# SyncE's transfers of the first stage: five under way at most, and a warm-up of two wide products

## The chip, the cores and the metric

One core of one Trainium2 chip runs the kernel. TensorE (PE in the profile, its weight loads PEld), VectorE (DVE), ScalarE (ACT) and GpSimd (POOL) compute; SyncE (SP) issues nearly all transfers, and sixteen DMA engines carry them. The metric is the device time of one execution in microseconds, lower is better.

## What is computed

A batch of 2 sequences of 3008 tokens with 256 features is filtered in the frequency domain, and two MLP layers follow, token by token. In float32:

```python
X = np.fft.rfft(x, axis=1)
y = np.fft.irfft(X * (filt_r + 1j * filt_i)[None], n=3008, axis=1)
t = y.reshape(6016, 256)
g = t @ w_gate                                    # 256 -> 1536
t = (g / (1 + np.exp(-g)) * (t @ w_val)) @ w_out  # 1536 -> 256
h = t @ w_in                                      # 256 -> 2048
out = (h * np.clip(h + 3, 0, 6) / 6) @ w_out2     # 2048 -> 256
```

The two MLPs' weights are held in float64; the kernel reads their words and makes float32 values of them.

## The kernel before

**Three stages on one core.** The first, about the first 72 us, is the Fourier part: 3008 = 47 x 64, so the transform is a product over 47 (`over_n1`), one over 64 (`over_n2`), the product with the filter (`filter_product`), and the way back over 64 (`back`); the way back over 47 (`to_time`) stands at the seam to the MLP. The second, to about 165 us, runs the first MLP for the first 1024 tokens, and meanwhile decodes its weights. The third, the rest, runs units of 7 products of 512 columns for the first MLP of the other tokens and then the second MLP.

**The first stage step by step.** It has 16 steps `STEPS`, each of 16 times 8 channels of one batch. Step k runs, in the order of the code, `over_n1(k)` (64 matmul records, line 332), `back(k-2)` (16 records, line 374), the transfers that `moves` holds for k, `over_n2(k)` (16 records, line 348) and `filter_product(k)` (four products on DVE, line 361, and four sums on POOL). `back(k-2)` needs those sums of step k-2. ACT takes results out of PSUM (lines 339, 340, 379). DVE also multiplies the filters' imaginary part by a sign (`prepare_filter`, line 324) and decodes the first weights (`Decode.part`, lines 196 to 209) between the steps.

**What SP issues in the first stage.** The matrices `mat`; the inputs `load_x(k)`, two transfers of 256 KB each into a ring of four places `ring`, issued three steps ahead; the filters `load_filter(j)`, two of 192 KB; the weights `load_dec(f)`, three of 256 KB or one of 768 KB; the results `store(b, a, i)`, 192 KB each from `turned` to the scratch `d2` in DRAM; and from there `load_half`, which brings back the halves that `form` turns to time (`g<-d`, `y<-d`, `turned<-d`). `load_x(0)` alone goes through ACT's queue. In the second stage `low_w1` stores decoded weights (`w1f<-x`) and `store` the other batch.

**What sets the order.** The engines' order is that of the code (a manual schedule). A transfer's landing is told by one of eight semaphores (DMAHW0 to DMAHW7) that are used in turn, so a transfer also waits until the eighth last has landed. SP takes its transfers in order: what stands behind a waiting one waits too.

**The warm-up.** Before the first input has landed, `idle(8)` multiplies a blank tile of 128 x 128 (line 317), which DVE has set to zero (line 311), eight times.

Of the kernel before, what the change touches and what calls it, by code (L numbers as in the profile page):

```python
# [16 lines left out]
P = 128  # L17
B, S, D = 2, 3008, 256
N1, N2 = 47, 64
N1P = 48  # L20
# [57 lines left out]
def fft_conv_glu_mlp(ctx: ExitStack, tc: tile.TileContext, x, filt, mats, sgn, w1, w2, out):  # L78
    nc = tc.nc
    w1, w2 = w1.bitcast(U32), w2.bitcast(U32)  # L80
# [9 lines left out]
    sg = keep.tile([P, NK], F32, name="sg")  # L90
# [7 lines left out]
    def wall(f):  # L98
        return wall_a[:, f] if f < 8 else wall_b[:, f - 8]


    d2 = [dram.tile([NK, P, D], F32, name=f"d2_{b}") for b in range(B)]
    yd = [dram.tile([P, 4, 512], F32, name=f"yd_{k}") for k in range(len(BLOCKS))]
    w1f = [dram.tile([P, 10 * P], F32, name=f"w1f_{f}") for f in range(F1)]
# [5 lines left out]
    def bank(tag="gv"):  # L110
        turn[tag] += 1
        return banks[tag][(turn[tag] - 1) % 4]

    def minus(out, a, b, engine=None):
        (engine or nc.vector).tensor_tensor(out=out, in0=a, in1=b, op=ALU.subtract)  # L115
# [9 lines left out]
    def rows(i, n=64):  # L125

        return slice(i * 64, i * 64 + n)
# [4 lines left out]
    def turns(first, n):  # L132

        return 32 * first // N1, -(-(32 * first + n // 2) // N1)
# [132 lines left out]
    with tc.manual_schedule():  # L267
# [7 lines left out]
        fl = [a[:, :3072].rearrange("p (j r n) -> p j r n", j=4, r=2) for a in (x0, side)]  # L275
        ring = work.tile([P, 7168], F32, tag="xs", name="ring")
        turned = work.tile([P, 7168], F32, tag="xs", name="turned")[:, :6144].rearrange("p (b q c) -> p b q c", b=2, c=P)
        room = new_y()

        N, RING = 16, 2  # L280
        STEPS = [(b, 4 * a + i) for a in range(2) for b in range(B) for i in range(4)]
        xin, first, spec, acc2 = {}, {}, {}, {}

        def load_x(k, engine=nc.sync):
            b, j = STEPS[k]
            if k % 2 == 0:
                xin[k // 2] = ring[:, k // 2 % RING * 2048:(k // 2 % RING + 1) * 2048].rearrange("p (a n) -> p a n", a=2)
            to, src = (v.rearrange("p (o i n) -> p i o n", o=2, i=2) if k < 2 else v.rearrange("p (i n) -> p i n", i=2)
                       for v in (xin[k // 2][:, k % 2], x[b, j // 2, :, j % 2]))
            for i in range(2):  # L290
                engine.dma_start(out=to[:, i], in_=src[:, i])

        def load_filter(j):
            for r in range(2):
                nc.sync.dma_start(out=fl[j // 4][:, j % 4, r], in_=filt[j][:, r])

        load_x(0, nc.scalar)
        load_x(1)
        nc.sync.dma_start(out=sg, in_=sgn)
        load_filter(0)  # L300
        load_filter(1)
        load_x(2)
        load_filter(2)
        load_x(3)
        load_filter(3)
# [1 line left out]
        nc.gpsimd.memset(warm, 0.0)  # L307
        nc.scalar.activation(out=warm, in_=warm, func=AF.Silu)

        blank = turned[:, 1, 0]  # L310
        nc.vector.memset(blank, 0.0)

        def idle(n):

            acc = bank()
            for _ in range(n):
                nc.tensor.matmul(acc[:, :P], blank, blank)

        idle(8)

        def prepare_filter(j):

# [57 lines left out]

        def store(b, a, i):
            q = slice(i * NK // 8, (i + 1) * NK // 8)
            nc.sync.dma_start(out=d2[b][q, :, a * P:(a + 1) * P].rearrange("q p c -> p q c"), in_=turned[:, b, q])  # L383

        def words(a):
            return a.bitcast(U32).rearrange("p (n t) -> p n t", t=2)
# [3 lines left out]
        def load_dec(f, n=1):  # L390
            a = x0[:, (f + 1) % 2 * 3072:]
            dec[f] = Decode(None, None, 768, (words(a[:, :1536]), a[:, 1536:2304], a[:, 2304:3072]))
            raw = dec[f].raw.rearrange("p n t -> p (n t)")
            for i in range(n):
                c = slice(1536 * i // n, 1536 * (i + 1) // n)
                nc.sync.dma_start(out=raw[:, c], in_=w1[:, f, c])

        def high_w1(f):
            nc.scalar.copy(out=wall(f)[:, 0], in_=dec[f].w)
# [1 line left out]
        def low_w1(f, engine=None):  # L401
            w = dec.pop(f).w
            minus(wall(f)[:, 1], w, wall(f)[:, 0].bitcast(F32), engine)
            nc.sync.dma_start(out=w1f[f][:, :6 * P], in_=w)

        todo = {}

# [9 lines left out]
        for k, f in ((1, 0), (8, 1), (11, 2)):  # L417
            send(k, load_dec, f, 3)
        for j in range(4, 8):
            send(j - 2, load_filter, j)  # L420
        for i in range(8):
            send((5, 5, 6, 6, 7, 7, 8, 8)[i], store, 0, 0, i)
            send((9, 9, 10, 10, 11, 11, 12, 12)[i], store, 1, 0, i)
            send(13, store, 0, 1, i)

        for f, steps in ((0, (4, 5, 5, 6, 7, 8, 9, 10, 10)), (1, (10, 11, 11, 12, 12, 13, 14, 15, 17)), (2, (15, 15, 15, 17))):
            at(steps[0], lambda f: dec[f].start(), f)
            for i in range(len(steps[1:7])):
                at(steps[1 + i], lambda f, i: dec[f].part(i, nc.vector), f, i)
            if f < 2:  # L430
                at(steps[7], high_w1, f)
                at(steps[8], low_w1, f)
            else:
                for i in range(3, 6):
                    at(N + 1, lambda f, i: dec[f].part(i, nc.vector), f, i)

        def load_half(j, a, g):
            t0, t1 = turns(FIRST[j][0], 512)
            g = g[:, :7 * P].rearrange("p (t c) -> p t c", c=P)
            for r in range(2):  # L440
                nc.sync.dma_start(out=g[rows(r, N1P), :t1 - t0],
                                  in_=d2[0].rearrange("q (h n) c -> (q h) n c", h=2)[:, 32 * r + t0:32 * r + t1, a * P:(a + 1) * P])
            return g

        half_accs = {}
# [17 lines left out]
        for k in range(N + 2):  # L463
            if 1 < k < N:
                over_n1(k)
            if 2 <= k <= N:
                back(k - 2)
            for step, *a in moves.get(k, ()):
                step(*a)
            if k == 12:  # L470
                g0 = new_g()
                gt[0] = [load_half(0, 0, g0)]
                gt[1] = [load_half(1, 0, room[:, 6 * COLS:])]
            elif k == N - 1:
                gt[0].append(load_half(0, 1, g0[:, 7 * P:]))
                gt[1].append(load_half(1, 1, turned[:, 0].rearrange("p q c -> p (q c)")))
            if k < N:
                over_n2(k)
                filter_product(k)
            elif k == N:  # L480
                for j in range(2):
                    form(j, 0)
                    form_end(j, 0)
            if k < 3 or 3 < k < 8:
                prepare_filter(k + (k < 3))
            for step in todo.get(k, ()) if k <= N else ():
                step()
# [80 lines left out]
        for t in range(2 * plain):  # L568
            p, i = divmod(t, 2)
            k, g_ = steps[p]  # L570
            f = 2 * g_ + i
# [8 lines left out]
            if t == 0:  # L580
                pairs = []
                for u in range(2):
                    if u:
                        back(N - 1)
                        turn["gv"] -= 2
                        for step in todo[N + 1][:3]:
                            step()
                        load_dec(3)
                        form(0, 1)
                        form_end(0, 1)  # L590
                        for step in todo[N + 1][3:]:
                            step()
                    pairs.append((bank(), bank()))
                    gate, val = pairs[u]
                    for part in ((0, 1, 2),) if u else ((0, 2), (1,)):
                        l1(gate, wall(u), (3 * P, 4 * P), xsd[k], part, depth=(0,))
                        l1(val, wall(u), (0, 5 * P), xsd[k], part, depth=(0,))
# [13 lines left out]
            h = hid[p][:, i]  # L611
# [10 lines left out]
            for f_ in part:  # L622
                low_w1(f_, nc.gpsimd)
                if f_ + 2 < F1:
                    load_dec(f_ + 2)
# [16 lines left out]
            if 10 < t < 23:  # L642
                q, r = divmod(t - 11, 2)
# [86 lines left out]
        class Plain:  # L730
            kind, k, f, n, last = 0, 0, 0, 512, True
# [125 lines left out]
        for s in range(S):  # L857
# [15 lines left out]
            k, f, n, kind = u.k, u.f, u.n, u.kind  # L873
# [121 lines left out]
```

## Time and profile before

| | us |
|---|---|
| median of 3 runs | 1123.38 |
| lowest and highest | 1122.09, 1124.87 |
| the profiled execution | 1120.58 |
| its span, first to last instruction | 1118.8 |

The profiled execution stands 2.80 us below the median of the runs, and 1.78 us of it lie outside its span. The views read below are: the page's busy times and its chain of work that ended last; tables by stretch of time, with each engine's busy time, the number of its instructions in brackets, TensorE's granted clock, the share of the sixteen DMA engines that was busy, and GB/s; the chain in order of time; the instructions in order of time, with the idle time before each and what ended it in square brackets ("issue": nothing that the profile shows); and the transfers, with the median time from issue to landing. The trace also tells packets that bring instructions to the engines, as queues q8 and q14.

### The profile page before, as it was taken

What the parts mean: (1) busy time and instruction counts of PE and PEld (TensorE: products, weight loads), DVE (VectorE), ACT (ScalarE), POOL (GpSimd) and SP (SyncE); (2) the same over time, 40 slices, a digit from 0 to 9 for tenths busy, and PEclk for the clock granted to TensorE, in tenths of its full rate; (3) what the DMA queues carried; (4) which work ended last, traced back from release to release, by engine and by line L of the source; (5) the groups of instructions that cost most, each with busy time, mean ns of one, the idle gap of its engine ahead of it and who ended that gap; (6) DMA issues with size and microseconds to landing.
All of it is one profiled execution on the core that took longest, in us unless ns stands there. A gap on an engine that the chain in (4) does not pass through costs nothing.

```text
span 1118.8 us, 19197 instructions
## 1 busy us (share of the span) xinstructions
PE 1108.6 (99%) x7246; PEld 924.9 (83%) x7246; DVE 858.3 (77%) x1168; ACT 751.9 (67%) x1367; POOL 602.3 (54%) x779
## 2 busy tenths in 40 slices
PE   9999999999999999999999999999999999999998
PEld 7678887888888888888899888888888888888997
DVE  5889976778878788786888868667677677677765
ACT  4554447667767667766777777777777677677764
POOL 4652375795765576484587645335435444354440
PEclk9999999999999999999999999999999999999999
DMA  9974954844633552263353421422322412412300
GB/s 315 296 210 132 278 186 157 223 152 134 200 118 111 147 176 100 83 202 104 102 208 120 162 82 60 153 78 71 135 78 78 144 62 78 149 52 77 117 27 33
DMA packets 58844, 150.75 MB, mean 135 GB/s; under 512 B 5568, under 2 KB 26016, under 8 KB 56992
## 3 DMA queue, kind: packets, MB, share of 16 engines
q1 hardware_dynamic: 58208, 149.01, 41.4%
q8 instruction: 56, 0.92, 0.3%
q10 hardware_dynamic: 544, 0.52, 0.2%
q14 instruction: 36, 0.29, 0.1%
HBM read 117.27 MB, written 32.24 MB: 134 GB/s over the span
## 4 chain that ended last, share of the span: by engine, by line
PE 94%; DVE 3%; DMA 1%; ACT 1%; issue 1%; SPq 0%; ACTq 0%; DVEq 0%
PE gv L680 44%; PE a L725 36%; PE gv L233 5%; PE a L241 2%; PE gv L374 2%; PE a L348 1%; PE gv L332 1%; PE gv L157 1%; DVE hs L115 1%; DVE h L707 1%; DVE xs L115 1%; DMA ring<-x_in 0%; DVE raw L115 0%; SPq L383 0%; DMA d<-turned 0%
## 5 line engine op out<-in xcount | busy, mean ns | idle before, releaser
L680 PE MATMUL gv<-xs,wu 128*128 128x512 f32 (+1 forms) x2268 | 567.1, 386 | 0.1
L115 POOL TENSOR_TENSOR wu<-st,wu 128x224 fp32r<-128x224 f32 x432 | 311.9, 753 | 397.0 <-ACT wu L517 397.0
L680 PEld LDWEIGHTS gv<-xs,wu 128*128 128x128 f32 x2268 | 423.7, 188 | 81.3 <-ACT raw L546 1.7
L725 PE MATMUL a<-hs,wo 128*128 128x512 f32 (+1 forms) x1872 | 476.7, 385 | 0.0
L725 PEld LDWEIGHTS a<-hs,wo 128*128 128x128 f32 x1872 | 351.4, 188 | 65.4 <-ACT hs L713 0.3
L115 DVE TENSOR_TENSOR hs<-h,hs 128x512 fp32r<-128x512 f32 (+3 forms) x228 | 235.4, 1033 | 66.8 <-ACT hs L713 62.3
L713 ACT CAST hs<-h 128x512 fp32r<-128x512 f32 (+3 forms) x216 | 172.6, 799 | 128.8 <-DVE h L709 73.9
L115 POOL TENSOR_TENSOR wo<-st,wo 128x256 fp32r<-128x256 f32 x156 | 148.8, 967 | 0.0
L709 DVE SCALAR_TENSOR_TENSOR h<-h,gv 128x512 f32<-128x512 f32 (+1 forms) x144 | 96.5, 670 | 22.7 <-ACT h L703 22.4
L517 ACT CAST wu<-st 128x384 fp32r<-128x384 f32 x216 | 110.6, 563 | 0.3 <-DMA st<-w1f 0.3
L701 ACT ACTIVATE h<-gv 128x512 f32<-128x512 f32 (+1 forms) x120 | 70.7, 589 | 58.3 <-PE gv L680 57.2
L118 DVE TENSOR_TENSOR gv<-gv,h 128x512 f32<-128x512 f32 (+1 forms) x108 | 74.0, 685 | 41.4 <-PE gv L680 35.7
L703 ACT ACTIVATE h<-gv 128x512 f32<-128x512 f32 (+1 forms) x144 | 84.1, 584 | 15.3 <-PE gv L680 15.1
L890 ACT COPY gv<-gv 128x512 f32<-128x512 f32 (+1 forms) x108 | 60.9, 564 | 42.6 <-PE gv L680 38.4
L118 DVE TENSOR_TENSOR h<-gv,h 128x512 f32<-128x512 f32 (+1 forms) x108 | 72.9, 675 | 18.5 <-PE gv L680 18.1
L709 DVE SCALAR_TENSOR_TENSOR h<-h,h 128x512 f32<-128x512 f32 (+1 forms) x48 | 32.7, 681 | 58.6 <-ACT h L703 58.6
L894 ACT COPY h<-gv 128x512 f32<-128x512 f32 (+1 forms) x108 | 62.5, 579 | 16.4 <-PE gv L680 13.4
L707 DVE TENSOR_TENSOR h<-h 128x512 f32<-128x512 f32 (+1 forms) x60 | 61.4, 1023 | 1.7 <-ACT h L701 1.0
L115 DVE TENSOR_TENSOR xs<-raw,xs 128x512 fp32r<-128x512 f32 (+1 forms) x77 | 58.9, 767 | 0.1
L517 ACT CAST wo<-st 128x256 fp32r<-128x256 f32 (+1 forms) x108 | 54.2, 501 | 0.0
L560 ACT CAST xs<-raw 128x512 fp32r<-128x512 f32 (+1 forms) x77 | 45.7, 609 | 2.9 <-DVE raw L115 2.8
L233 PE MATMUL gv<-xs,wall_a 128*128 128x512 f32 x192 | 45.7, 392 | 0.1
(88 smaller groups left out, 899.7 us busy)
## 6 DMA issues: line engine op xcount, KB each, us to landing
st<-w1f SPq DMA_DIRECT2D x60, 576.0 KB, 3.8
st<-w2f SPq DMA_DIRECT2D x48, 704.0 KB, 4.1
raw<-w_in SPq DMA_DIRECT2D x16, 512.0 KB, 4.6
ring<-x_in SPq DMA_DIRECT2D x30, 256.0 KB, 5.5
x<-w_in SPq DMA_DIRECT2D x9, 768.0 KB, 5.4
d<-turned SPq DMA_DIRECT2D x32, 192.0 KB, 5.3
yd<-y SPq DMA_DIRECT2D x5, 1024.0 KB, 6.5
raw<-yd SPq DMA_DIRECT2D x5, 1024.0 KB, 6.3
```

Source lines behind the costliest of these rows:

```text
L115: (engine or nc.vector).tensor_tensor(out=out, in0=a, in1=b, op=ALU.subtract)
L118: (engine or nc.vector).tensor_tensor(out=out, in0=a, in1=b, op=ALU.add)
L233: nc.tensor.matmul(acc, w[:, r, c[k]:c[k] + P], xs[:, v, k], start=(r, v, k) == (0, 0, 0), stop=(r, k) == (1, 1), skip_group_check=len(dep ...
L517: nc.scalar.copy(out=to[:, 0, at:at + hi - lo], in_=src[:, lo:hi])
L680: nc.tensor.matmul(acc[:, :n], w[:, r, FORM[a] * P:(FORM[a] + 1) * P], xs_part(k, v, i), start=start and q == 0, stop=q == 2, skip_group_c ...
L701: nc.scalar.activation(out=self.value(t, 0), in_=src, func=AF.Silu)
L703: nc.scalar.activation(out=self.value(t, a), in_=src, func=AF.Relu, bias=3.0)
L707: nc.vector.tensor_tensor(out=self.value(t, 0), in0=self.value(t, 0), in1=src, op=ALU.mult)
L709: nc.vector.scalar_tensor_tensor(out=self.value(t, a), in0=self.value(t, a), scalar=6.0, in1=src, op0=ALU.min, op1=ALU.mult)
L713: nc.scalar.copy(out=self.hs[:, t, :, 0, :self.n], in_=self.value(t))
L725: yield lambda t=t, v=v, a=a, j=j, r=r: nc.tensor.matmul(banks["a"][2 * j + t][:, :n], self.wo[:, r, (2 * a + j) * P:(2 * a + j + 1) * P], ...
L894: nc.scalar.copy(out=u.s7, in_=b3[:, :n])
```

## The change

Every transfer of the first stage, and of `low_w1`, `load_dec` and `store` in the second, now goes through a helper `move`. If SP issues it, and five or more went through `move` before, it also waits for the landing of the fifth last of these. Transfers of the later stages (line 183, `load_g`, `ask_unit`, `put_y` and the output), and that of `mat`, don't go through it. The warm-up multiplies a blank tile of 128 columns by 512 columns, twice; DVE sets 128 x 512 to zero for it.

```diff
-        N, RING = 16, 2
+        N, RING, MOST_UNDER_WAY = 16, 2, 5
+        under_way = []
+
+        def move(to, src, engine=nc.sync):
+
+            ins = engine.dma_start(out=to, in_=src)
+            if engine is nc.sync:
+                if len(under_way) >= MOST_UNDER_WAY:
+                    tc.add_manual_dep(ins.ins, under_way[-MOST_UNDER_WAY].ins.name,
+                                      mybir.DependencyInfo(mybir.DependencyClass.Sync, mybir.DependencyReason.DATA),
+                                      reason="few transfers under way")
+                under_way.append(ins)
...
             for i in range(2):
-                engine.dma_start(out=to[:, i], in_=src[:, i])
+                move(to[:, i], src[:, i], engine)
...
-        blank = turned[:, 1, 0]
+        blank = turned[:, 1, 0:4].rearrange("p q c -> p (q c)")
         nc.vector.memset(blank, 0.0)
...
             for _ in range(n):
-                nc.tensor.matmul(acc[:, :P], blank, blank)
+                nc.tensor.matmul(acc, blank[:, :P], blank)
 
-        idle(8)
+        idle(2)
```

In the same way `nc.sync.dma_start` becomes `move` in `load_filter`, for `sg`, and in `store`, `load_dec`, `low_w1` and `load_half`. No engine's instructions change places but for the warm-up's.

On SP, early in the first stage: the transfers of filters 1 and 2 and of inputs 2 and 3 (`x_122` is the tile of the filters, `ring` that of the inputs). Before:

```order
5 L295 DMA x_122<-filt_in 128x384 [waits DMAHW0_49]
6 L295 DMA x_122<-filt_in 128x384 [waits DMAHW1_49]
7 L291 DMA ring<-x_in 128x512 [waits DMAHW2_49]
8 L291 DMA ring<-x_in 128x512 [waits DMAHW3_49]
9 L295 DMA x_122<-filt_in 128x384 [waits DMAHW4_49]
```

And now, where line 285 is that of `move`:

```order
5 L285 DMA x_122<-filt_in 128x384 [waits DMAHW2_49,DMAHW0_49]
6 L285 DMA x_122<-filt_in 128x384 [waits DMAHW4_49,DMAHW1_49]
7 L285 DMA ring<-x_in 128x512 [waits DMAHW5_49]
8 L285 DMA ring<-x_in 128x512 [waits DMAHW6_49,DMAHW3_49]
9 L285 DMA x_122<-filt_in 128x384 [waits DMAHW7_49]
```

Each now waits for a semaphore three turns younger than before: filter 1 for the two halves of input 1, input 2 for `sg` (DMAHW5) and for filter 0 (DMAHW6).

On SP, at the end of the first stage: the last of the loads of step 12, the eight stores of step 13, and the loads of step 15 that need them. Before:

```order
76 L441 DMA y<-d_0_79 48x6x128 [waits DMAHW7_49]
77 L383 DMA d_0_79<-turned 128x3x128 [waits DMAHW0_49,Activation_49]
78 L383 DMA d_0_79<-turned 128x3x128 [waits DMAHW1_49]
79 L383 DMA d_0_79<-turned 128x3x128 [waits DMAHW2_49]
80 L383 DMA d_0_79<-turned 128x3x128 [waits DMAHW3_49]
81 L383 DMA d_0_79<-turned 128x3x128 [waits DMAHW4_49]
```

And now:

```order
76 L285 DMA y<-d_0_79 48x6x128 [waits DMAHW2_49]
77 L285 DMA d_0_79<-turned 128x3x128 [waits DMAHW3_49,Activation_49]
78 L285 DMA d_0_79<-turned 128x3x128 [waits DMAHW4_49]
79 L285 DMA d_0_79<-turned 128x3x128 [waits DMAHW5_49]
80 L285 DMA d_0_79<-turned 128x3x128 [waits DMAHW6_49]
81 L285 DMA d_0_79<-turned 128x3x128 [waits DMAHW7_49]
```

The second to the fifth store (rows 78 to 81) waited for transfers before the four loads; now they wait for those loads themselves, the second for the first `g<-d` and the fifth for the last `y<-d`.

## Rows read from the trace of the kernel before

**Rows 1.** The page: the chain that ended last, by engine.

```profile
PE 94%; DVE 3%; DMA 1%; ACT 1%; issue 1%; SPq 0%; ACTq 0%; DVEq 0%
```

**Rows 2.** Busy time by stretch: length, PE, PEld, DVE, ACT, POOL, clock, DMA share, GB/s.

```profile
25.00:43.00 18.00, 17.44 (x430) 13.31 (x426) 16.41 (x26) 9.97 (x29) 13.69 (x20) 1.00 0.96 310
43.00:56.00 13.00, 10.55 (x270) 7.99 (x268) 8.71 (x15) 7.32 (x19) 7.70 (x13) 1.00 0.93 286
80.00:1119.00 1039.00, 1034.03 (x5483) 866.66 (x5481) 799.20 (x1068) 709.13 (x1256) 556.60 (x710) 1.00 0.38 124
```

**Rows 3.** The chain in order of time, 10 to 60 us: start, length, what.

```profile
11.54 0.86 issue
...
27.67 0.25 issue
...
33.25 0.31 issue
...
43.54 1.06 issue
...
49.95 1.39 issue
```

**Rows 4.** Instruction packets, 27.91 to 44.60 us: queue, packets, MB, share of 16 engines.

```profile
q8 instruction: 3, 0.05, 1.1%
```

**Rows 5.** Busy time by stretch, as in rows 2, between the chain's gaps and packets.

```profile
27.91:44.60 16.68, 15.31 (x382) 11.79 (x382) 15.91 (x27) 8.46 (x24) 12.34 (x17) 1.00 0.94 295
42.23:44.60 2.37, 1.31 (x53) 1.03 (x46) 1.87 (x5) 0.21 (x1) 1.68 (x3) 1.00 0.59 167
49.02:51.34 2.31, 0.93 (x8) 0.13 (x1) 2.11 (x3) 1.19 (x4) 2.17 (x3) 1.00 0.97 329
62.84:65.77 2.93, 2.93 (x94) 2.76 (x90) 2.55 (x5) 1.46 (x5) 2.49 (x4) 1.00 0.88 240
```

**Rows 6.** Instructions in order of time, 0 to 16 us: start, length, engine, line.

```profile
0.83 0.17 DVE L311 MEMSET turned<- 128x128 f32 x1 [0.83 <-PEq L980]
1.05 3.78 PE L317 MATMUL gv<-turned 128*128 128x128 f32 x16 [1.05 <-DVE turned L311]
...
4.76 1.11 PE L332 MATMUL gv<-mat,ring 48*64 48x48 f32 x32
6.17 1.61 PE L332 MATMUL gv<-mat,ring 48*64 48x48 f32 x96 [0.30 <-DMA ring<-x_in]
...
10.55 0.86 PEld L332 LDWEIGHTS gv<-mat,ring 48*64 48x64 f32 x43 [0.21 <-DMA ring<-x_in]
...
13.31 0.52 PEld L374 LDWEIGHTS gv<-h,mat 64*64 64x64 f32 x10 [0.36 <-POOL h L118]
```

**Rows 7.** Transfers issued at 2.2, 3.0 and 6.2 us: number, size, median us to landing.

```profile
sg<-sgn_in SPq DMA_DIRECT2D x1, 12.0 KB, 4.9
...
x<-filt_in SPq DMA_DIRECT2D x2, 192.0 KB, 4.7
...
ring<-x_in SPq DMA_DIRECT2D x2, 256.0 KB, 4.1
```

**Rows 8.** The same, of 14 to 26 us, and of 145 to 152 us.

```profile
ring<-x_in SPq DMA_DIRECT2D x8, 256.0 KB, 5.4
...
w1f<-y SPq DMA_DIRECT2D x2, 256.0 KB, 2.0
```

**Rows 9.** In order of time, 58 to 78 us, and landings of transfers from 60 and 68.3 us.

```profile
60.29 5.43 SPq L383 DMA_DIRECT2D d<-turned  x8
...
68.36 0.82 SPq L441 DMA_DIRECT2D g<-d  x2
...
74.84 0.84 PE L157 MATMUL a<-mat,g 48*64 48x47 f32 x48
...
d<-turned SPq DMA_DIRECT2D x8, 192.0 KB, 3.6
...
g<-d SPq DMA_DIRECT2D x2, 144.0 KB, 3.2
```

More of the change, by code (lines that the diff above doesn't have):

```diff
@@ L290, in load_x @@
             for i in range(2):
-                engine.dma_start(out=to[:, i], in_=src[:, i])
+                move(to[:, i], src[:, i], engine)
         def load_filter(j):
             for r in range(2):
-                nc.sync.dma_start(out=fl[j // 4][:, j % 4, r], in_=filt[j][:, r])
+                move(fl[j // 4][:, j % 4, r], filt[j][:, r])
         load_x(0, nc.scalar)
         load_x(1)
-        nc.sync.dma_start(out=sg, in_=sgn)
+        move(sg, sgn)
         load_filter(0)
@@ L382, in store @@
             q = slice(i * NK // 8, (i + 1) * NK // 8)
-            nc.sync.dma_start(out=d2[b][q, :, a * P:(a + 1) * P].rearrange("q p c -> p q c"), in_=turned[:, b, q])
+            move(d2[b][q, :, a * P:(a + 1) * P].rearrange("q p c -> p q c"), turned[:, b, q])
         def words(a):
@@ L395, in load_dec @@
                 c = slice(1536 * i // n, 1536 * (i + 1) // n)
-                nc.sync.dma_start(out=raw[:, c], in_=w1[:, f, c])
+                move(raw[:, c], w1[:, f, c])
         def high_w1(f):
@@ L403, in low_w1 @@
             minus(wall(f)[:, 1], w, wall(f)[:, 0].bitcast(F32), engine)
-            nc.sync.dma_start(out=w1f[f][:, :6 * P], in_=w)
+            move(w1f[f][:, :6 * P], w)
         todo = {}
@@ L440, in load_half @@
             for r in range(2):
-                nc.sync.dma_start(out=g[rows(r, N1P), :t1 - t0],
-                                  in_=d2[0].rearrange("q (h n) c -> (q h) n c", h=2)[:, 32 * r + t0:32 * r + t1, a * P:(a + 1) * P])
+                move(g[rows(r, N1P), :t1 - t0], d2[0].rearrange("q (h n) c -> (q h) n c", h=2)[:, 32 * r + t0:32 * r + t1, a * P:(a + 1) * P])
             return g
```

## The prediction

> **What bounds the kernel now.** First the chain of work that ended last: 94% of it is TensorE [rows 1]. Then the stretches, because the change touches only one of them. From 80 us on TensorE is busy for 1034.03 of 1039.00 us [rows 2]; the change adds no work there and takes none away, so a microsecond that the first stage gains or loses stays to the end, as long as TensorE stays the bound. So the first stage alone is to be read. Its chain, in order of time, has five gaps under "issue", time in which TensorE had work and waited for nothing that the profile shows: 0.86, 0.25, 0.31, 1.06 and 1.39 us, 3.87 us together [rows 3]. That sum is all that a cure of these gaps could return.
>
> What are they? Between the ends of the second and the fourth gap, at 27.91 and 44.60 us, three packets of instructions of some 16 KB each came over queue q8 [rows 4], and TensorE ran 382 products and 382 weight loads [rows 5]: about 255 instructions to a packet (I count 256), so gaps end where a block ends. In the stretch from a packet's start to the end of its gap (packets begin at 42.23 and 49.02 us, where two of the stretches begin) the gap ends 2.37 and 2.31 us after that start [rows 5]. I read the gaps as waits for the next block. With few transfers in the way it comes in time: in the stretch that begins with a packet at 62.84 us, among the eight stores, TensorE still had 184 instructions ahead of it and did not stop; with a full queue 99 were left at 42.23 us and 9 at 49.02 us [rows 5].
>
> The Trainium skill says the same less sharply: its page "Runtime: NRT & Kernel Launch", section "Instruction fetch mechanics", has the next block of 256 instructions fetched while the present one runs, and calls the cost of a crossing mostly hidden. The trace agrees from 80 us on and shows 3.87 us that aren't hidden before; by the page the change could return nothing, by the row up to that sum.
>
> **The limit of five.** Before, there was a limit already: with eight semaphores in turn each transfer waited for the landing of the eighth last. So the step is from eight to five, not from no limit. Transfers of 14 to 26 us took 5.4 us to land [rows 8]; with eight under way that is 0.68 us for each. What does a shorter queue cost? A transfer of 256 KB that had the engines nearly to itself landed after 2.0 us [rows 8], and the eight stores, some five of which were under way at a time, after 3.6 us [rows 9]. Five under way therefore give one in 0.40 to 0.72 us; I take the store's row, as the nearest, less a little for its small pieces: 0.66 us, the rate of today. The engines stay full and landings keep their pace. Each transfer is issued later and is under way for a shorter time.
>
> Where a load has no margin, this shows. Input 2 is the closest: it was issued at about 6 us and landed 4.1 us later [rows 7], and TensorE waited 0.21 us for it at 10.55 us [rows 6]. Now its halves wait for `sg`, issued at 2.2 us and landing 4.9 us later, at 7.1 us, and for filter 0, issued at 2.7 and 3.4 us and landing after 4.7 us, at 7.4 us and later [rows 7]. Issued at 7.3 and 7.8 us with fewer ahead of it, it lands 3.0 to 3.3 us later, at 10.3 to 11.1 us: up to 0.6 us later than now. What hides that is POOL: `back(0)`, behind it on TensorE, stood until 13.31 us for a sum of POOL [rows 6], and that sum hangs on input 0 and filter 0, which are not moved. The 64 records of `over_n1(2)`, about 1.1 us, would still end at some 12.2 us. Cost 0; without that cover, 0.6 us. For the same reason the first gap (0.86 us, ending at 12.39 us) gives nothing back.
>
> At the end of the stage, the second to the fifth store now wait for the four loads before them. The stores are issued from 60.29 us on; the loads of what they wrote begin at 68.36 us and land 3.2 us later, about 72.2 us with the second's issue, while the product that uses them starts at 74.84 us [rows 9]: a margin of 2.7 us. The stores are held up by half a microsecond at most; if TensorE comes 1.8 us earlier, 0.4 us of margin is left. Cost 0, and 0.5 us if the loads take longer. Behind the waiting SP stand only transfers of steps that are later still, with inputs issued three steps ahead.
>
> **What comes back of the gaps.** With five under way the packet should come as at 62.84 us, with 184 of 256 instructions left, not 99: 85 instructions earlier, at 16.68 us for 764 of them [rows 5] 1.9 us. I halve this, since the stores' queue is lighter than one of inputs and filters: 0.9 us earlier.
> - The gaps of 0.25 and 0.31 us go. But from 25 to 43 us DVE is busy for 16.41 of 18.00 us [rows 2], so it becomes the next to hold TensorE: I count 0.2 of 0.56 us.
> - The gap of 1.06 us shrinks to 0.16: 0.9 us back. DVE is busy for 8.71 of 13.00 us from 43 to 56 us [rows 2] and follows.
> - The gap of 1.39 us: its block was asked for just after 44.60 us, behind a stretch in which the DMA engines were only 0.59 busy [rows 5], so a full queue was not all of it. I count half, 0.7 us.
>
> Together 0.2 + 0.9 + 0.7 = 1.8 us; the bounds are 0 and 3.87 us.
>
> **The warm-up.** The columns are the same, 8 x 128 or 2 x 512, and so is the work: 3.78 us [rows 6], less some fixed cost of 16 records against 4. The tile to be zeroed is four times as wide, 0.17 to at most 0.68 us [rows 6], so the warm-up ends 0 to 0.5 us later. The 32 products that follow it take 1.11 us from 4.76 us, and then TensorE stands 0.30 us until 6.17 us for the other half of input 0 [rows 6], which comes over ACT's queue and isn't moved. The products before 6.17 us take twice as long each as those after (1.11 us for 32, 1.61 for 96), so the clock rises about there from 1.2 to 2.4 GHz, although the granted clock of the stretches shows 1.00 [rows 2]; the same work before it should raise it at the same time. Cost 0, at most 0.2 us.
>
> Fewer records also mean 24 fewer instructions on TensorE (16 + 16 before, 4 + 4 now), so each block ends 24 instructions further on in the program. With 96 products and 96 weight loads in a step, 256 instructions are a step and a third: the block that ends inside `over_n1` is short, the others are longer by what of `back` or `over_n2` is in them. Moved by 24, the block before it becomes short too, by my count of the steps 4.7 us instead of 5.6.
>
> **Rivals.** *The depth of the queue doesn't matter to an instruction packet.* For it: the last gap, and that landings differ little. Then packets come as late as now, the gaps stay, and the newly short block before `over_n1(9)` adds up to 0.8 us, while the long one at 50 us gives some 0.6 back: 1120.58 + 0.2, in the median 1123.6 us. Against it: the packet at 62.84 us. On this the Trainium skill, page "DMA: Bandwidth & Descriptors", section "Queues, rings and completion order", says that each DMA engine goes round the queues that have work, packet by packet. By that rule a packet of instructions would stand behind one data packet, however many transfers are queued, and this rival would hold; the gaps, which come only in the loaded stage, speak against it.
>
> *All of it comes back, and some more*, since ACT's and DVE's own packets come earlier too: 3.4 to 4.5 us, in the median 1119 to 1120 us. Against it: POOL and DVE as next bounds.
>
> *Five are too few (slower).* From about 8 us to the loads at 68.36 us [rows 9] 80 transfers land (counted in the order), one in 0.75 us. If a transfer's landing takes more than 5 x 0.75 = 3.8 us with five under way, the transfers of the first stage set its end, at the inputs of `over_n1` and at the stores before 68.36 us. Each 0.1 us above that costs 80 x 0.02 = 1.6 us. At 4.2 us it is 6.4 us, less the margins of 2.7 us: 1120.58 + 3.7, in the median 1127 us. For it: one slow engine of the sixteen holds a landing, and now holds the queue sooner. Against it: 3.6 and 2.0 us [rows 8, 9].
>
> **How the numbers follow.** Chances: gaps partly closed 0.50, depth without effect 0.22, more than all gaps 0.18, five too few 0.10. The likeliest gives 1120.58 - 1.8 = 1118.8 us against the profiled execution; that stood 2.8 us below the median, so 1121.6 us is predicted for the median. Medians of so few runs move by a microsecond. The range of 1118.0 to 1125.5 us takes in the first two cases and nearly all of the third, and leaves out the slower one. A measurement can tell about 0.3%, 3.4 us, from no change: faster than 1120.0 us is most of the third case and an edge of the first, 0.22; slower than 1126.8 us is the last, 0.10; between them lie 0.68.
>
> **What would show it.** In the chain after: the gaps of 43.5 and 50 us gone or under half, at places 24 instructions further on; the median landing of inputs near 3.3 us instead of 5.4; the MLP's first product (line 233 before) some 1.8 us earlier; DVE above 91% busy from 25 to 43 us. Wrong it is if gaps stay as long while landings shorten (depth without effect), if TensorE waits for inputs at several steps or for `g<-d` (five too few), or if products after 6.2 us still take the longer time (the clock).

## The result, and the profile after

The change makes the kernel slower, by 0.77%. In one series with the kernel before, after takes 1130.12 us in the median (1127.22 to 1131.21, 6 runs) and before 1121.63 us (1119.87 to 1124.87, 6 runs): a ratio of 1.0077, 95% interval 1.0058 to 1.0095. The profiled execution took 1127.22 us with a span of 1125.4 us, 6.6 us more than before in both; the medians differ by 8.5 us.

The page's chain, by engine, answers to [rows 1]: transfers, 1% before, are now 5% of it, TensorE 92%.

```profile
PE 92%; DMA 5%; DVE 1%; ACT 1%; issue 0%; POOL 0%; SPq 0%; DVEq 0%; ACTq 0%
```

**All of it is lost in the first stage.** The last piece of that stage on TensorE is the product that brings `turned` back to time (line 157), at the seam to the first MLP. The row tells the shortest, median and longest product in ns and the start of the first and the last in us; first before, then after:

```profile
L157 PE MATMUL a<-mat,turned x48: 214/232/235, 78.6 to 79.3; 48*64 48x47 f32 x32, 48*64 48x26 f32 x8, 48*64 48x42 f32 x8
```

```profile
L157 PE MATMUL a<-mat,turned x48: 214/232/235, 85.1 to 85.8; 48*64 48x47 f32 x32, 48*64 48x26 f32 x8, 48*64 48x42 f32 x8
```

It begins 6.5 us later, and the span is 6.6 us longer: next to nothing is lost behind it. In all 13 profiled kernels of this study the span is 1039.5 to 1040.9 us longer than that start, whatever its place (78 to 115 us), so the start is a measure of the stage from here on.

**The transfers no longer keep up.** After by stretch of time (length, busy us and number of instructions of PE, PEld, DVE, ACT and POOL, TensorE's granted clock, DMA share, GB/s), as [rows 2]:

```profile
10.00:25.00 15.00, 13.95 (x330) 9.95 (x326) 9.94 (x19) 7.20 (x21) 9.94 (x16) 1.00 0.86 276
25.00:43.00 18.00, 17.64 (x466) 13.71 (x464) 16.90 (x29) 10.30 (x30) 12.74 (x19) 1.00 0.84 250
43.00:56.00 13.00, 9.67 (x200) 7.55 (x194) 6.87 (x11) 6.08 (x16) 7.00 (x11) 0.83 0.88 268
56.00:72.00 16.00, 16.00 (x388) 12.57 (x384) 13.15 (x22) 8.12 (x25) 10.45 (x15) 0.92 0.93 273
```

From 25 to 43 us the DMA engines are busy for 0.84 of the time and move 250 GB/s, where before they were busy for 0.96 and moved 310 [rows 2]. Each transfer does land sooner, 4.4 us instead of 5.4 [rows 8] (before has 5.5 if read from 4 to 60 us, as after is here), but five in 4.4 us is one in 0.88 us, and eight in 5.4 us were one in 0.68. Transfers of after issued from 4 to 60 us, with the median time to landing:

```profile
ring<-x_in SPq DMA_DIRECT2D x26, 256.0 KB, 4.4
x<-w_in SPq DMA_DIRECT2D x9, 256.0 KB, 4.1
d<-turned SPq DMA_DIRECT2D x12, 192.0 KB, 4.4
side<-filt_in SPq DMA_DIRECT2D x8, 192.0 KB, 4.3
```

**The chain shows who sets the pace.** Its pieces in order of time, start and length, 25.9 to 81 us of after:

```profile
25.94 0.07 PE gv L344 x3
26.01 5.30 DMA ring<-x_in
31.32 0.02 issue
31.33 4.24 DMA side<-filt_in
...
35.63 4.67 DMA ring<-x_in
...
40.33 5.23 DMA d<-turned
...
45.62 4.32 DMA x<-w_in
...
67.41 3.40 DMA g<-d
...
74.49 2.71 DMA d<-turned
...
77.64 3.61 DMA g<-d
```

From 26 us on there is no compute in it: a transfer lands, less than 0.1 us later SP issues the one that is fifth behind it, which lands after 2.7 to 5.3 us, and so on, up to the loads `g<-d`, issued at 77.28 us where before they were at 68.36 [rows 9]. Before, this chain was TensorE with five gaps from 6 to 58 us [rows 3]. The rows of the prediction end at 60 us, and there the chain of before goes over to the eight stores, a landing and a load:

```profile
60.29 0.38 SPq L383
...
65.17 3.10 DMA d<-turned
...
68.36 2.42 DMA g<-d
```

So transfers were near the limit at the end of the stage already, though TensorE's weight loads stood for only 0.23 us there, until 71.91 us.

What TensorE waited for in after from 8 to 80 us (total us, times, longest) is not even large, because the wait reaches it through others: POOL's sum stands for the products that had no input.

```profile
PE gv L386 <- POOL h L118: 2.6, 1, 2.6
PE gv L344 <- issue: 1.0, 2, 0.7
PE gv L386 <- POOL h L115: 1.0, 1, 1.0
```

The wait that ends last before the seam is for the loads themselves, just behind that window. In square brackets is the idle time and what ended it:

```profile
80.10 0.31 PE L157 MATMUL a<-mat,g 48*64 48x47 f32 x2 [0.21 <-DMA g<-d]
81.30 0.89 PE L157 MATMUL a<-mat,g 48*64 48x47 f32 x46 [0.89 <-DMA g<-d]
```

In and after the 2.6 us, which end at 52.37 us, TensorE's clock is at its lower level: the granted clock of the stretch from 51.65 to 58.47 us is 0.50, 1.2 of 2.4 GHz.

```profile
51.65:58.47 6.82, 6.10 (x63) 4.73 (x63) 1.26 (x2) 4.46 (x10) 0.67 (x2) 0.50 0.99 301
```

### The profile page after: what moved, and what is told of

It reads as the page before. It is cut to its first block, busy times and chain, and to the rows that moved or that the text cites. A ratio compares the mean times of both kernels' runs of the same rounds, so it can differ in the third digit from the quotient of the medians.

```text
span 1125.4 us, 19173 instructions
## 1 busy us (share of the span) xinstructions
PE 1113.0 (99%) x7234; PEld 924.7 (82%) x7234; DVE 857.6 (76%) x1168; ACT 752.3 (67%) x1367; POOL 602.2 (54%) x779
## 4 chain that ended last, share of the span: by engine, by line
PE 92%; DMA 5%; DVE 1%; ACT 1%; issue 0%; POOL 0%; SPq 0%; DVEq 0%; ACTq 0%
PE gv L691 45%; PE a L736 37%; PE gv L233 4%; PE a L241 2%; DMA ring<-x_in 2%; DMA d<-turned 1%; PE gv L157 1%; DMA x<-w_in 1%; PE gv L344 1%; DMA g<-d 1%; PE a L360 1%; PE gv L386 0%; DMA side<-filt_in 0%; PE gv L329 0%; DVE h L630 0%
```

## The experiments

All kernels of this section compute the whole result. Each ratio is against runs of before on the same chip in the same series (medians 1120.75, 1121.25 and 1120.14 us for the three series).

### One part at a time: the warm-up alone, the limit alone

**e1_warm_only** has the two wide products and no limit, **e2_limit_only** the limit of five and the old warm-up.

```diff
 e1_warm_only
-        blank = turned[:, 1, 0]
+        blank = turned[:, 1, 0:4].rearrange("p q c -> p (q c)")
...
-                nc.tensor.matmul(acc[:, :P], blank, blank)
+                nc.tensor.matmul(acc, blank[:, :P], blank)
...
-        idle(8)
+        idle(2)
 e2_limit_only
+        N, RING, MOST_UNDER_WAY = 16, 2, 5
...
+                if len(under_way) >= MOST_UNDER_WAY:
+                    tc.add_manual_dep(ins.ins, under_way[-MOST_UNDER_WAY].ins.name,
```

> The warm-up of the change alone: two products of 512 columns, a tile of 128 x 512 set to zero; SP's transfers as before. In the changed kernel the clock rose at 10.7 us, not at 6.1 us, and back(0) began at 14.44 us, not 12.76. Theory A (two losses: the queue of five is the large one, the late clock a small one): the first 128 records of over_n1 take 3.7 us again, back(0) comes some 1.7 us later, the gaps stay about as before, and the time is 1 to 2.5 us above the kernel before (ratio 1.001 to 1.002). Theory B (the late clock is the loss, and the idle times and the second fall of the clock follow from it): 6 to 8 us above, ratio 1.005 to 1.007. Theory C (the rise is chance from run to run and has nothing to do with the warm-up): ratio 1.000 and a rise near 6 us.

> The limit of five alone, with the warm-up of before. Theory A: landings of inputs take 4.2 to 4.9 us with five under way, one in some 0.87 us, the DMA engines are busy for 0.84 to 0.88 of 10 to 56 us, TensorE waits for inputs' consequences from 43 us on, and the time is 4 to 7 us above the kernel before (ratio 1.004 to 1.006). Theory B: at most 1 us above, ratio 1.000 to 1.001, since the clock rises at 6 us.

Measured: the warm-up alone 1120.82 us, ratio 0.9998 (0.9988 to 1.0008); the limit alone 1128.74 us, ratio 1.0070 (1.0055 to 1.0085). The limit is the whole loss, a little more than the 0.4 to 0.6% that were expected of it, and the warm-up is worth nothing that can be told either way. The seam's product begins at 79.3 us with the warm-up alone and at 88.0 us with the limit alone:

```profile
L157 PE MATMUL a<-mat,turned x48: 214/232/235, 79.3 to 80.0; 48*64 48x47 f32 x32, 48*64 48x26 f32 x8, 48*64 48x42 f32 x8
```

```profile
L157 PE MATMUL a<-mat,turned x48: 214/232/235, 88.0 to 88.7; 48*64 48x47 f32 x32, 48*64 48x26 f32 x8, 48*64 48x42 f32 x8
```

### Does the warm-up's form hold the clock back?

After and e2 both showed products at the slower pace for longer than before, which seemed to make a second cause. **e3_wide_early** has two products of 512 columns that read the blank 128 columns four times, so that DVE's zeroing stays short and they start at 1.05 us; **e4_narrow_late** has the old eight products behind the long zeroing, starting at 1.45 us. Neither has a limit.

```diff
 e3_wide_early
-                nc.tensor.matmul(acc[:, :P], blank, blank)
+                nc.tensor.matmul(acc.rearrange("p (q c) -> p q c", q=4), blank, blank.unsqueeze(1).to_broadcast([P, 4, P]))
...
-        idle(8)
+        idle(2)
 e4_narrow_late
-        nc.vector.memset(blank, 0.0)
+        nc.vector.memset(turned[:, 1, 0:4].rearrange("p q c -> p (q c)"), 0.0)
```

> The kernel before with a warm-up of two products of 512 columns whose tile is only 128 columns wide (its columns are read four times over), so that setting it to zero takes 0.17 us as before and the warm-up begins at 1.05 us. It tells the shape of the warm-up from its start. If the form (few wide products, four weight loads instead of sixteen) makes the clock rise late: rise near 10.7 us, ratio 1.001 to 1.002. If the start 0.4 us later does: rise near 6.1 us, ratio 1.000.

> The kernel before with its eight products of 128 columns, but with 128 x 512 set to zero first, so that the warm-up begins at 1.45 us. If the later start makes the clock rise late: rise near 10.7 us, ratio 1.001 to 1.002. If the form does: rise near 6.1 us, ratio 1.000.

Measured: e3 1121.42 us, ratio 1.0013 (0.9999 to 1.0026); e4 1121.28 us, ratio 1.0004 (0.9992 to 1.0016). The profiles, TensorE's instructions from about 4.8 us on, first e3, then e4, then e2, whose warm-up is that of before to the letter:

```profile
4.84 1.10 PE L332 MATMUL gv<-mat,ring 48*64 48x48 f32 x32
6.35 2.81 PE L332 MATMUL gv<-mat,ring 48*64 48x48 f32 x96 [0.40 <-DMA ring<-x_in]
```

```profile
4.98 0.68 PE L332 MATMUL gv<-mat,ring 48*64 48x48 f32 x32
6.19 1.61 PE L332 MATMUL gv<-mat,ring 48*64 48x48 f32 x96 [0.53 <-DMA ring<-x_in]
```

```profile
6.22 2.81 PE L344 MATMUL gv<-mat,ring 48*64 48x48 f32 x96 [0.35 <-DMA ring<-x_in]
```

The 96 products take 1.61 us at the one pace and 2.81 us at the other. The old warm-up shows both (before and e4 short, e2 long), and so does the wide one (e1 short at 6.29 us, after and e3 long). So neither the form nor the start of the warm-up decides it in these executions. The limit may have a part in it: of the 13 profiles, all four with a limit of five from the first transfer on (after, e2, e6 and e8_five_first) are long, and of the nine others only e3 and e5_limit_7. No run separates that from chance. What the slow start costs isn't shown by itself either. In e3 it puts `back(0)` at 14.46 us (12.76 before), yet the seam's product begins at 77.8 us, the earliest of all; but in that execution the gaps under "issue" are 3.1 us shorter than before, too, and the interval of e3's ratio reaches 1.0026.

### How does the time go with the depth?

**e5_limit_3, e5_limit_6 and e5_limit_7** are e2 with another number.

```diff
-        N, RING, MOST_UNDER_WAY = 16, 2, 5
+        N, RING, MOST_UNDER_WAY = 16, 2, 3    # 6, 7
```

> The limit at three, warm-up of before. The theory after the first runs: a transfer has a fixed time that no other shares, so a short queue leaves the DMA engines idle; inputs landed after 5.4 us with eight under way (one in 0.68 us) and 4.4 us with five (one in 0.88 us), on a line that is 2.7 us and 0.33 us for each under way. At three: 3.7 us to land, one in 1.24 us; the 88 transfers to the end of the first stage then take some 109 us instead of 77 with five, and the time is 35 to 45 us above the kernel before (ratio 1.03 to 1.04). Rival (what costs is only that SP stands behind waits, while the engines are as full as before): landing in 2.0 to 2.5 us, ratio 1.007 to 1.012.

> The limit at six, warm-up of before. By the line: 4.7 us to land, one in 0.79 us, 88 transfers in 69.5 us, about what the stage takes now (68.4 us to the loads after the last store); ratio 1.000 to 1.003. If the loss came from waits on SP and not from idle engines, it would fall evenly from five to eight: ratio 1.004 to 1.005.

> The limit at seven, warm-up of before. By the line: 5.1 us to land, one in 0.72 us; the stage is no longer bound by transfers, and instruction packets come no later than with eight: ratio 0.998 to 1.001. By the rival of an even fall: 1.002 to 1.003.

Measured, with the depth of 8 that the semaphores of before impose. Landing is the median of `ring<-x_in` issued from 4 to 60 us; the share of the DMA engines and GB/s are those of 10 to 25 us; the seam is the start of the product on `turned`.

| under way | landing us | landing / depth | DMA share | GB/s | seam us | median us | ratio (95%) |
|---|---|---|---|---|---|---|---|
| 3 | 3.9 | 1.30 | 0.64 | 193 | 114.5 | 1156.87 | 1.0317 (1.0298 to 1.0335) |
| 5 | 4.4 | 0.88 | 0.81 | 255 | 88.0 | 1128.74 | 1.0070 (1.0055 to 1.0085) |
| 6 | 4.8 | 0.80 | 0.91 | 291 | 79.7 | 1124.49 | 1.0024 (1.0015 to 1.0032) |
| 7 | 5.4 | 0.77 | 0.94 | 310 | 79.9 | 1121.36 | 0.9995 (0.9987 to 1.0004) |
| 8 | 5.5 | 0.69 | 1.00 | 346 | 78.6 | | 1 |

The stretch from 10 to 25 us, of depth 3, 5, 6, 7 and 8, columns as above:

```profile
10.00:25.00 15.00, 11.26 (x246) 7.58 (x242) 9.53 (x19) 4.29 (x12) 7.69 (x13) 0.89 0.64 193
```

```profile
10.00:25.00 15.00, 14.74 (x314) 10.03 (x310) 9.95 (x19) 6.86 (x21) 9.55 (x16) 1.00 0.81 255
```

```profile
10.00:25.00 15.00, 14.52 (x374) 10.92 (x370) 11.03 (x23) 7.74 (x21) 10.15 (x17) 1.00 0.91 291
```

```profile
10.00:25.00 15.00, 13.96 (x340) 10.05 (x334) 9.94 (x19) 7.69 (x22) 9.93 (x16) 1.00 0.94 310
```

```profile
10.00:25.00 15.00, 14.14 (x375) 11.10 (x371) 11.03 (x23) 7.81 (x21) 10.23 (x17) 1.00 1.00 346
```

From eight to three under way the landing falls by 1.6 us of 5.5, not to three eighths. So a good part of it does not depend on what else is queued, and with few under way the engines stand idle during that part; the rate falls in step. The time doesn't fall in step: seven costs nothing that can be told, six 0.24%, five 0.70%, three 3.2%. That rules out the rival of an even fall, which asked for 0.4 to 0.5% at six. Between seven and six the reserve of the stage is used up. The profiled execution of six has its seam at 79.7 us, no later than seven's, so the 0.24% is seen in the runs and not in that one profile, which at 1121.77 us is the fastest of the eleven runs; one execution scatters by a microsecond or two.

With six there is another thing to read. What TensorE waited for from 8 to 80 us, first before, then depth 6:

```profile
PE gv L332 <- issue: 2.2, 3, 1.1
PE gv L374 <- issue: 1.7, 2, 1.4
```

```profile
PE gv L386 <- ACT turned L391: 1.4, 1, 1.4
PE a L157 <- DMA g<-d: 1.1, 2, 0.9
PE a L360 <- ACT y L351: 0.4, 1, 0.4
PE gv L344 <- DMA ring<-x_in: 0.3, 1, 0.3
PE gv L386 <- POOL h L118: 0.3, 1, 0.3
```

The gaps under "issue" are gone from this view; before they were 3.9 us of it, and all of it (1.7 and 2.2 us). In their place stand 3.5 us of other waits, and the seam gained nothing.

### Is it the number of transfers, or the bytes under way?

**e6_whole_5** keeps the limit of five and makes most transfers two or three times as large: inputs 2 to 15 in one transfer of 512 KB, filters of 384 KB, first weights of 768 KB, stores in pairs of 384 KB. **e7_whole_8** is the same with eight.

```diff
+            if k > 1:
+                move(xin[k // 2][:, k % 2], x[b, j // 2, :, j % 2], engine)
+                return
...
-            for r in range(2):
-                nc.sync.dma_start(out=fl[j // 4][:, j % 4, r], in_=filt[j][:, r])
+            move(fl[j // 4][:, j % 4], filt[j])
...
-            q = slice(i * NK // 8, (i + 1) * NK // 8)
+            if i % 2:
+                return
+            q = slice(i * NK // 8, (i + 2) * NK // 8)
...
-            send(k, load_dec, f, 3)
+            send(k, load_dec, f, 1)
```

> The limit at five, but inputs 2 to 15, filters, first weights and stores go as whole transfers (512, 384, 768 and 384 KB) and no longer as two or three parts; warm-up of before. If bytes under way are what counts, five of these hold the engines as full as ten of the others: DMA share back at 0.95 and more from 10 to 43 us, first product of the MLP at 71 to 73 us, ratio 0.999 to 1.002. If a limit of five hurts whatever the size (SP waits, later issue): ratio 1.004 to 1.008.

> Inputs 2 to 15, filters and first weights as whole transfers (512, 384, 768 KB) and the stores in pairs (384 KB), with the limit set to eight, which the eight semaphores impose anyway; warm-up as before. This is the control of e6_whole_5 (limit five, same sizes, 1.0012). Theory (what counts is the bytes under way): five large transfers already fill the DMA engines, so eight give no more than e6: ratio 0.998 to 1.002, and what e6 lost against before is the coarser arrival, which stays. Rival (the number of transfers counts for itself, whatever their size): eight large ones come back to 0.996 to 0.999, visibly below e6_whole_5.

Measured: e6 1123.01 us, ratio 1.0012 (1.0000 to 1.0025); e7 1122.82 us, ratio 1.0019 (1.0009 to 1.0028). The stretch from 10 to 25 us of e6 and of e7, and the landings of the inputs (4 to 60 us) of e6 and of e7:

```profile
10.00:25.00 15.00, 13.96 (x346) 10.02 (x341) 10.01 (x20) 7.27 (x20) 9.93 (x16) 1.00 0.98 371
```

```profile
10.00:25.00 15.00, 12.53 (x304) 9.01 (x300) 9.49 (x19) 6.78 (x19) 9.92 (x16) 1.00 0.96 368
```

```profile
ring<-x_in SPq DMA_DIRECT2D x14, 512.0 KB, 6.2
```

```profile
ring<-x_in SPq DMA_DIRECT2D x14, 512.0 KB, 7.4
```

With the same limit of five, twice the bytes keep the engines busy for 0.98 of the time, against 0.81, and 5.8 parts in a thousand of the 7.0 come back. Twice the bytes land in 6.2 us, not in 2 x 4.4. And with this size eight under way are no better than five, in time or in GB/s: the depth no longer matters. Two things of the expectation for e6 did not come: from 25 to 43 us the share of the engines is 0.87, not 0.95, and the first product of the MLP is at 74.8 us, not at 71 to 73. What stays, 0.1 to 0.2%, both have, so it isn't the limit's; what it is was not tested. Coarser pieces, which come whole or not at all, are one possibility. Another stands in the traces: the gaps under "issue" from 8 to 80 us are 4.5 us in e6 and 6.1 us in e7, against 3.9 before.

### Where in the stage does it cost?

**e8_five_first** limits SP's first 40 transfers of the stage and leaves the rest to the eight semaphores, **e8_five_last** the other way round; sizes and warm-up as before. Before, transfer 40 was issued at about 27 us.

```diff
 e8_five_first
-                if len(under_way) >= MOST_UNDER_WAY:
+                if MOST_UNDER_WAY <= len(under_way) < 40:
 e8_five_last
-                if len(under_way) >= MOST_UNDER_WAY:
+                if len(under_way) >= 40:
```

> The limit of five for the first 40 of SyncE's transfers alone, none after; sizes and warm-up as before. Theory (the rate is lost all along, and the need catches up with the transfers from about 26 us on): the 40th transfer, issued at 27 us before, comes 4 to 6 us later, and eight under way catch up only where they have slack (transfers 58 to 61 found three under way before): ratio 1.001 to 1.004, about half of 1.007. Rival one (only the last stores and what follows them count): 1.000. Rival two (the early inputs alone count): 1.006 to 1.008.

> No limit for the first 40 of SyncE's transfers, five from the 41st on; sizes and warm-up as before. Theory (rate lost all along): the second half starts as before, 47 transfers at 0.88 us for 0.72 us cost up to 7 us, less the slack: ratio 1.002 to 1.005, and with e8_five_first about the sum 1.007. Rival one (only the last stores and what follows them count): 1.006 to 1.008. Rival two (the early inputs alone count): 1.000.

Measured: first 1123.83 us, ratio 1.0029 (1.0017 to 1.0040); last 1123.69 us, ratio 1.0028 (1.0015 to 1.0040). Each half costs the same, and their sum, 0.57%, lies inside the interval of the whole limit (0.55 to 0.85%). Neither the early inputs nor the last stores alone carry it; the loss comes in both halves of the stage. The seams' rows, first and last:

```profile
L157 PE MATMUL a<-mat,turned x48: 214/232/235, 83.8 to 84.5; 48*64 48x47 f32 x32, 48*64 48x26 f32 x8, 48*64 48x42 f32 x8
```

```profile
L157 PE MATMUL a<-mat,turned x48: 214/232/235, 83.1 to 83.7; 48*64 48x47 f32 x32, 48*64 48x26 f32 x8, 48*64 48x42 f32 x8
```

## Why the prediction was wrong, step by step

Predicted were 1121.6 us, with a range of 1118.0 to 1125.5; measured were 1130.12 us. The sum added 2.8 us to the profiled execution, its distance from a median of three runs; with the six runs of before it is 1.05 us, so the forecast itself would have been about 1119.9 us. That widens the miss and doesn't explain it.

**TensorE bounds, and only the first stage counts: right.** The span followed the start of the seam's product within 1.4 us in all 13 profiles.

**The step that failed is "The limit of five … 0.66 us, the rate of today. The engines stay full".** It measured 0.88 us for a transfer (4.4 us for five), against the bounds of 0.40 and 0.72 us. Both rows that bounded it were misread:
- The stores' 3.6 us [rows 9] are of transfers of 192 KB, the inputs' of 256 KB. Time per transfer was taken for a rate. In bytes the same row speaks against the step: 0.72 us for 192 KB is 273 GB/s, where the loaded stage moved 310 and 286 [rows 2]. The stretch of the stores, with some five under way, even shows it outright, at a DMA share of 0.88 and 240 GB/s [rows 5]. After moved 250 to 276.
- The lone write's 2.0 us [rows 8] says that part of a landing is there with nothing else under way. Divided by five it was taken as a rate that five can reach; it is rather the part that fewer transfers can't shorten. With depths of 3, 5, 6, 7 and 8 landings were 3.9, 4.4, 4.8, 5.4 and 5.5 us.

The Trainium skill has the sum that the step lacked: its page "DMA: Bandwidth & Descriptors", section "Anatomy of one DMA — SWDGE (gpsimd) path", gives a transfer some 2.0 us that don't depend on its size, and its bytes at 436 GB/s, a fit for transfers that GpSimd prepares. An estimate by that page, with the bytes of all transfers under way in its second term (2.0 us and five times 262 kB), comes to 5.0 us for five inputs, 3.8 for three and 6.8 for eight. The runs show 4.4, 3.9 and 5.5: it is near for few and too high for many, and it would have put five above the break-even of 3.8 us.

**The rival "Five are too few" came true, near its price.** Its break-even was a landing of 3.8 us, and each 0.1 us above it 1.6 us. At the measured 4.4 us that is 9.6 us, less the margins of 2.7: 6.9 us. The profiles give 6.6 us and the medians 8.5; for the limit alone they give 9.3 and 8.0, at the same landing of 4.4 us. The margin is borne out: the loads `g<-d` began 8.9 us later and the seam 6.5, so 2.4 us were taken up. The mechanism and the sum stood there; what was wrong was the chance of 0.10, which rested on the rows just named. The experiments bear the mechanism out: depth, bytes, and each half of the stage.

**"Cost 0" for input 2 and for the stores: the times were wrong, for the first the cost was right.** Input 2's halves landed 4.3 and 4.4 us after their issue, at 11.5 and 12.2 us and not at 10.3 to 11.1; TensorE was still busy with earlier products until then, at the slow pace, and did not wait for them. `back(0)` began at 14.44 us instead of 12.76 for that pace, and not for input 2. The stores ended 8.9 us late, not "half a microsecond at most": that figure took landings of 3.2 us as given and counted no delay from the stage before them.

**"What comes back of the gaps", 1.8 us:** the gaps did shrink as the step says, from 3.87 us to 0.36 and 0.69 us in after, and to none that this view shows with six. The sign for DVE was seen too: it was busy for 16.90 of 18.00 us from 25 to 43 us, 0.94. But nothing was gained. With six the time was 0.24% worse, and waits of 3.5 us stood in the gaps' place. The step's fault is to count a gap that closes as time won, though DVE was named as next. In e3, at full depth, the gaps are 3.1 us shorter than before and the seam is 0.8 us earlier, one execution each. Whether the depth closed the gaps is not settled either. From 8 to 80 us TensorE stood under "issue" for 3.9, 3.8, 3.1 and 0.8 us at full depth (before, e1, e4, e3), for 1.8 with seven, none with six, 1.0 and 1.5 with five (after, e2), 1.0 and 1.2 with five in one half, none with three, and with the large transfers for 4.5 (five) and 6.1 us (eight). First e3, then e6 and its second kind:

```profile
PE gv L332 <- issue: 0.8, 2, 0.4
```

```profile
PE gv L346 <- issue: 4.2, 3, 1.5
PE gv L388 <- issue: 0.3, 1, 0.3
```

That runs with the bytes under way but for e3, and with few under way TensorE waits for other things, behind which a late packet wouldn't show. So the rival of depth without effect can't be dismissed; its rule of packets in turn was neither shown nor refuted here.

**The warm-up, cost 0: right** (0.9998, 0.9988 to 1.0008). Its reason, that the same work raises the clock at the same time, is not what the profiles show: the products come to the faster pace by 6.2 us in some executions and after 9 us in others, with either warm-up. The sign "products after 6.2 us still take the longer time" was seen and meant nothing for the time.

**What stays open.** In after, TensorE ran at 1.2 GHz from 51.65 to 58.47 us, after it had stood for want of work; the first 16 products after the wait took 3.12 us, where 16 of the same line at 45.86 us took 1.52. No run separates what that adds from what the late transfers cost by themselves, since the stretch comes from the late transfers. For little speak that the chain holds transfers alone there, and that TensorE waited for `g<-d` once more at 81.30 us, so that it was ahead of the transfers by then.

## What to carry to other kernels

A limit on transfers under way is a limit on bytes under way. Before you set one, multiply depth by size, divide by the landing time at that depth (measured, or bounded by a row of the same size), and compare the GB/s with what the stage moves now; compare rates, never times per transfer of different size. If the depth has to be small, make the transfers larger: five of double size cost 0.12% here where five small ones cost 0.70%. And a gap that closes in a chain is not yet time won: look for the next wait behind it, which here stood close.

## What the hardware showed that was not expected

- The landing time of 256 KB grows slowly with the depth, 3.9 us with three under way and 5.5 us with eight, so that it takes about seven transfers of 192 to 256 KB (some 1.6 MB) to lose nothing that can be told here; five of 384 to 768 KB lose 0.12%.
- The moment at which TensorE's first products come to the faster pace isn't fixed by the warm-up. The 96 products of `over_n1` at 6.2 to 6.4 us took 1.61 or 2.81 us in different executions, with the same warm-up, and the times of the kernels don't sort by it.
